# A fused attention-and-MoE kernel: the first output block of batch 0 is 8 chunks long, its weight product is made between output bursts, and no fetch slot is set

## The chip, the cores and the metric

The kernel runs on one core of one Trainium2 chip. The metric is device time in microseconds (us); runs of one kernel are summed up by their median. A span is the time from the first to the last instruction of the program in the one execution that was profiled.

## What is computed

`x` is (4, 12544, 128) in float32, `inducing` is (32, 128), `moe_w1` and `moe_w2` are (128, 1024), `moe_w_out` is (1024, 128). Cut to what matters, the reference is:

```python
def mab(q, kv):                       # per batch
    s = (q @ kv.transpose(0, 2, 1)) / sqrt(128)
    a = exp(s - s.max(-1)); a /= a.sum(-1) + 1e-9
    return a @ kv
h = mab(inducing, x)                  # (4, 32, 128): 32 queries over 12544 rows
y = mab(x, h).reshape(50176, 128)     # every row over the 32 rows of h
out = maximum(y @ w1, y @ w2) @ w_out # (50176, 128), float32
```

The kernel writes maximum(a, b) as a + relu(b - a): the part with w1 alone needs only the product w1*w_out (128x128), and the relu part needs h*(w2 - w1).

## The kernel before, in words

**Units and stages.** A batch is 98 chunks of 128 rows. Batch 0 has a stage of its own: its rows are loaded in ten units (16, 16, 16, 16, 8, 8, 8, 4, 4, 2 chunks) by DMAs that the POOL queue issues. For each unit `u_transpose` (T) makes TensorE transposes (L239) and copies them to `xT` (L244, L247), `u_scores` (S) makes exp of the scores with `inducing` (L204 to L222 for units 0 to 2, L258 and L269 for the others), and `u_accum` (A) sums the weights (L284) and the weighted rows (L293). The order of T, S and A in TensorE's queue is written out by hand for the last units. `u_h` then turns the sums into h: `sum_part` (L317), a small matmul (L324), hT4 (L334), the reciprocal rs (L343). In between stand eight transposes of w1 (L304) with their copy to `w1T` (L311). `u_hwd` makes h*(w2 - w1) in four slices of 256 columns (L441), copied out by ACT (L463) and DVE (L454) in turns.

**Blocks, bursts, finals.** Output rows are made in blocks of 16, 8, 4 or 2 chunks. `Block.stage` makes exp of the block's scores with h (L532, L542). A block is one or two parts, and a part has one to four bursts. A burst (`Part.burst`, L597) is 8 or 16 matmuls into four PSUM buffers and four relu copies (L628 on DVE, L632 on ACT). A final (`Part.final`, L659) is 16 matmuls with w_out into one PSUM buffer, with the small product `m1` opened ahead of them (L612, where a part has two column tiles) or behind them (L668), and a scaling copy on DVE into an output tile `o` (L685). Two finals fill one `o` tile (one in a block of 2 chunks); the second of them issues the tile's store to DRAM (L695), on POOL's queue for batches 0 to 2. There are four `o` tiles in turn, so the copy into a tile waits until the store from that tile four stores earlier has landed.

**The loop.** All bursts of all batches are numbered g = 0, 1, ... In step g the loop issues burst g, stages the blocks that are due, issues the oldest final that is queued, and then the jobs that are due at g. A part's finals are queued behind its last burst. Batch 0 has 49 bursts and 49 finals. From g = 7 on, final f (counted from 0) is issued in step g = f + 4.

**Which engine copies, which buffer is used.** `Model` keeps estimated times while the program is written down: it chooses the PSUM buffer that comes free first and the engine (DVE or ACT) for each relu copy. The result is a fixed order in each engine's queue.

**Jobs beside batch 0's output.** In step 9 `transpose_batch(1)` puts a one-element copy in POOL's queue (L135, waits for batch 1's last load) and seven DMA transposes of batch 1's rows in SP's queue (L129), which wait for that copy. In steps 14, 18, 22, ... `p1_scores(1, i)` (L357) reads the i-th transposed part. In step 24 `hold_loads` puts a one-element copy in POOL's queue (L143, waits for the last DMA transpose), and steps 24, 26, 28, ... put the loads of batch 2 behind it (L120), in the same queue as the stores.

**Instruction fetch.** Ahead of the fifth final, `addr_align(256, offset=174)` sets at which of 256 instruction slots TensorE's program goes on.

Of the kernel before, what the change touches and what calls it, by code (L numbers as in the profile page):

```python
# [9 lines left out]
F16 = mybir.dt.float16  # L10
# [41 lines left out]
def kernel(  # L52
# [23 lines left out]
    for i, (_, n) in enumerate(p1_blocks):  # L76
# [4 lines left out]
        else:  # L81
            units.append((i, 0, n))
    NU = len(units)
    last = NU - 4

    consts = ctx.enter_context(tc.tile_pool(name="consts", bufs=1))
# [62 lines left out]
    ones32 = consts.tile([128, 128], F32, name="ones32")  # L149
    ones16 = consts.tile([128, 1], F16, name="ones16")  # L150
    same_m = consts.tile([128, 4, M], F32, name="same_m")
    sum_scale = consts.tile([128, 2], F32, name="sum_scale")

    warm = consts.tile([128, 512], F16, name="warm")
# [11 lines left out]
    with tc.manual_schedule(engines={ET.PE, ET.DVE, ET.Activation, ET.Pool, ET.SP}):  # L166
# [28 lines left out]

        st = [dict() for _ in range(B)]

        def col_scores(b, k0, n, name):


            bi, ps = bank([128, P1B * M])
            for q in range(4):
                r = slice(32 * q, 32 * (q + 1))
                nc.tensor.matmul(  # L204
                    out=ps[r, 0 : n * 32],
                    lhsT=inducingT,
                    rhs=xT_tiles[b % 2][:, k0 : k0 + n, r],
                    start=True,
                    stop=True,
                    tile_position=(0, 32 * q),  # L210
                )
            end = model.pe(32 * n / 2400, model.bank_free[bi], "col")
            eT = eTp.tile([128, P1B * M], F16, name=f"eT_{name}", tag="eT")
            nc.scalar.activation(
                out=eT[:, 0 : n * M], in_=ps[:, 0 : n * M], func=AF.Exp, scale=scale
            )
            model.bank_free[bi] = model.ev("ACT", n * M, end)
            return eT, model.bank_free[bi]
# [11 lines left out]
        def u_transpose(i):  # L230
            t, g0, n = units[i]
            xn = xn_of(0, t)
            step = 8
            for g in range(g0, g0 + n, step):
                m = min(step, g0 + n - g)
                bi, ps = bank([128, 8, 128], F16)
                end = 0.0
                for j in range(m):
                    nc.tensor.transpose(ps[:, j, :], xn[:, g + j, :], identity16)  # L239
                    end = model.pe(0.056)  # L240
                k = p1_blocks[t][0] + g
                dst = xT_tiles[0][:, k : k + m, :]
                if i >= last - 2 or (g // step) % 2 == 0:
                    nc.vector.tensor_copy(out=dst, in_=ps[:, 0:m, :])  # L244
                    model.bank_free[bi] = model.ev("DVE", 64 * m, end)
                else:
                    nc.scalar.copy(out=dst, in_=ps[:, 0:m, :])  # L247
                    model.bank_free[bi] = model.ev("ACT", 128 * m, end)

        def u_scores(i):  # L250
            t, g, n = units[i]
            k = p1_blocks[t][0] + g
            if i < 3:
                pool0["et", i], _ = col_turn(*col_scores(0, k, n, f"0_{i}"), n, f"0_{i}")
                return
            bi, ps = bank([128, P1B * M])
            for j in range(n):
                nc.tensor.matmul(  # L258
                    out=ps[:, j * M : (j + 1) * M],
                    lhsT=xT_tiles[0][:, k + j, :],  # L260
                    rhs=inducingT,
                    start=True,
                    stop=True,
                )
                end = model.pe(0.025, model.bank_free[bi])
            et = etp.tile([128, P1B, M], F16, name=f"et_0_{i}", tag="et")
            if n % 4:
                nc.vector.memset(et[:, n : n + 4 - n % 4, :], 0.0)
            nc.scalar.activation(  # L269
                out=et[:, 0:n, :], in_=ps[:, 0 : n * M], func=AF.Exp, scale=scale  # L270
            )
            model.bank_free[bi] = model.ev("ACT", n * M, end)
            pool0["et", i] = et

        def u_accum(i):
            t, g, n = units[i]
            et = pool0.pop(("et", i))
            xn = xn_of(0, t)
            if i == 0:
                for name in ("h", "sum"):  # L280
                    pool0[name] = bank([128, 512])
                    model.bank_free[pool0[name][0]] = 1e9
            for j in range(0, n, 4):
                nc.tensor.matmul(  # L284
                    out=pool0["sum"][1][:, 0:1],
                    lhsT=et[:, j : j + 4, :],
                    rhs=ones16,
                    start=(i == 0 and j == 0),
                    stop=(i == NU - 1 and j + 4 >= n),
                )  # L290
                model.pe(0.025)
            for j in range(n):
                nc.tensor.matmul(  # L293
                    out=pool0["h"][1][:, 0:M],
                    lhsT=xn[:, g + j, :],
                    rhs=et[:, j, :],
                    start=(i == 0 and j == 0),
                    stop=(i == NU - 1 and j == n - 1),
                )
                model.pe(0.025)  # L300

        def w1T_transpose(bi, ps, jbs):
            for jb in jbs:
                nc.tensor.transpose(  # L304
                    ps[:, jb, :], w1h[:, 128 * jb : 128 * (jb + 1)], identity16
                )
                end = model.pe(0.056, model.bank_free[bi])
            return end

        def w1T_evict(bi, ps, end):  # L310
            nc.vector.tensor_copy(out=w1T, in_=ps)  # L311
            model.bank_free[bi] = model.ev("DVE", 512, end)

        def u_h():

            part = smp.tile([128, 2], F32, name="sum_part")
            nc.vector.tensor_mul(  # L317
                part, pool0["sum"][1][:, 0:1].broadcast_to((128, 2)), sum_scale
            )
            end = model.ev("DVE", 2, model.t["PE"], 0.1)  # L320
            bi, ps = pool0["sum"]
            w1T_bank = bank([128, NJB, 128], F16)
            w1T_transpose(*w1T_bank, range(NJB // 2))
            nc.tensor.matmul(  # L324
                out=ps[:, 0:2],
                lhsT=same_m.rearrange("p q m -> p (q m)"),
# [2 lines left out]
                stop=True,  # L329
            )  # L330
            end = model.pe(0.1, end)
            w1T_end = w1T_transpose(*w1T_bank, range(NJB // 2, NJB))
            hT4 = smp.tile([C, 4, M], F16, name="hT4_0", tag="hT4")
            nc.vector.tensor_scalar(  # L334
                out=hT4,
# [9 lines left out]
            hT4 = hT4.rearrange("c q m -> c (q m)")  # L345
            neg = smp.tile([C, 128], F16, name="hT4n")
            nc.scalar.mul(neg, hT4, -1.0)
            w1T_evict(*w1T_bank, w1T_end)
            st[0]["hT4"], st[0]["neg"] = hT4, neg
            st[0]["rs"], st[0]["scale"] = rs[:, 0:1], rs[:, 1:2]  # L350

# [75 lines left out]
        def u_hwd():  # L427
# [22 lines left out]
            for i, (bi, ps) in enumerate(banks):  # L450
                end = ends[i]
                sl = slice(w * i, w * (i + 1))
                if i % 2:
                    nc.vector.tensor_scalar(  # L454
                        out=hwd[:, sl],
                        in0=ps[:, 0:w],
# [242 lines left out]
        def blocks_of(b):  # L699
# [4 lines left out]
                sizes.append(s)  # L704
                rest -= s
            if b == 0:
                sizes = [2, 4, 8] + sizes[:-1]
                sizes[-1] = K - sum(sizes[:-1])
                last = sizes.pop()
                while last:  # L710
                    s = 8 if last >= 8 else 4 if last >= 4 else 2
                    sizes.append(s)
                    last -= s
# [34 lines left out]
            model.bank_free[bi] = model.ev("DVE", 128, end)  # L748


        for i in range(last - 1):
            u_transpose(i)
            if i >= 1:
                u_scores(i - 1)
            if i >= 2:
                u_accum(i - 2)
            if i < last - 2:
                keep_warm(1)
        u_transpose(last - 1)
        u_scores(last - 2)  # L760
        u_accum(last - 3)
        u_transpose(last)
        u_scores(last - 1)
        u_accum(last - 2)
        u_transpose(last + 1)
        u_scores(last)
        u_transpose(last + 2)
        u_accum(last - 1)
        u_scores(last + 1)
        u_transpose(last + 3)  # L770
        u_scores(last + 2)
        u_accum(last)
        u_scores(last + 3)
        for i in range(last + 1, NU):
            u_accum(i)
        for i in range(NP1):
# [10 lines left out]
        stages = {}  # L787
        for b in range(B):
            blks = [blk for blk in flat if blk.b == b]
            lead_in = 3 if b == 0 else 0  # L790
            for i, blk in enumerate(blks):
                j = i if i < lead_in else i - (i - lead_in) % 2
                stages.setdefault(max(-1, first[blks[j].name] - 3), []).append(blk)
        stages[-1][0].stage()
        u_hwd()
        for blk in stages[-1][1:]:
            blk.stage()
        prep_w1out()

        jobs = {}  # L800

# [31 lines left out]
            at(33 + 2 * i, sub_w, i)  # L833

        queue = []
        nfinal = 0
        for g, (p, u) in enumerate(seq):
            lead = []
            if len(queue) > 1 and queue[0][0].tn == 2 and queue[0][1] % 2 == 0:
                lead = queue[0:2]  # L840
            p.burst(u, lead)
            if g == 0:
                small_m1(0)
            for blk in stages.get(g, ()):
                blk.stage()
            if queue:
                if nfinal == 4:

                    nc.tensor.addr_align(256, offset=174, max_nops=0)
                nfinal += 1  # L850
                part, *a = queue.pop(0)
                part.final(*a)
            if u == 0 and p.t0 == 0:
# [39 lines left out]
```

## Time and profile before

| what | value |
|---|---|
| median of 7 runs | 338.3 us (337.82 to 339.77) |
| profiled execution: its time | 339.77 us |
| profiled execution: its span | 338.0 us |
| PE busy | 329.9 us, 98% of the span |
| DVE busy / ACT busy | 299.0 us / 271.8 us |
| relu copy on ACT / on DVE, 128x512 | 602 ns / 681 ns |
| scaling copy to `o`, 128x256 | 419 ns |
| DMA transposes of a batch | 21 in three batches, median 7.4 us from issue to landing |

PE is TensorE's matmul row, DVE VectorE, ACT ScalarE, POOL GpSimd and SP SyncE. In a line of the timeline the columns are the start in us from the span's start, the duration in us, the engine, the line of the kernel, the operation, what is written <- what is read, the shape and the count; in brackets stands how long the engine was idle before and what released it. A "q" behind an engine's name is its queue. In the chain of waits a line is start, duration and what the chain stood on.

### The profile page before, as it was taken

How to read it: one execution, taken by the hardware profiler on the slowest of the kernel's cores; microseconds unless marked ns; L12 is line 12 of the kernel's file. 1: busy time of each engine (PE TensorE's matmuls, PEld its weight loads, DVE VectorE, ACT ScalarE, POOL GpSimd, SP SyncE). 2: the span in 40 equal slices, each digit the busy share in tenths (PEclk: the TensorE clock that was granted, in tenths of full speed). 3: DMA queues.
4: the chain of work that ended last, by engine and by line, in shares of the span. 5: the costliest groups of instructions: out<-in, count | busy, mean ns of one | idle time of the engine just before them, and what ended most of it. 6: DMA issues, size and time to landing. Idle time of an engine off the chain costs nothing.

```text
span 338.0 us, 14462 instructions
## 1 busy us (share of the span) xinstructions
PE 329.9 (98%) x6316; PEld 262.5 (78%) x6316; DVE 299.0 (88%) x632; ACT 271.8 (80%) x523; POOL 94.5 (28%) x166
## 2 busy tenths in 40 slices
PE   8999999999999999999999999999999999999995
PEld 3776787887878878888777878888777778878875
DVE  0668999998989999999998999999998998999993
ACT  3648978777898887787899877787899989888881
POOL 6332113175741234543341232332242100000000
PEclk9999999999999999999999999999999999999999
DMA  7999799999929996994229992221221221222222
GB/s 213 208 208 214 179 200 201 203 248 222 270 104 203 212 221 145 180 252 151 81 85 172 229 248 69 97 89 70 96 96 66 106 99 68 95 95 95 96 97 109
DMA packets 54143, 51.47 MB, mean 152 GB/s; under 512 B 41536, under 2 KB 42464, under 8 KB 54080
## 3 DMA queue, kind: packets, MB, share of 16 engines
q0 software_dynamic: 11552, 32.38, 37.6%
q1 hardware_dynamic: 42528, 18.17, 26.7%
q8 instruction: 49, 0.80, 1.0%
q14 instruction: 14, 0.11, 0.1%
HBM read 28.33 MB, written 25.69 MB: 160 GB/s over the span
## 4 chain that ended last, share of the span: by engine, by line
PE 90%; DMA 3%; DVE 3%; ACT 2%; issue 1%; POOL 0%; POOLq 0%; DVEq 0%
PE ps L659 55%; PE ps L597 18%; PE ps L612 4%; DMA out_dram<-o 3%; PE ps L191 2%; PE ps L532 2%; PE ps L357 2%; PE ps L379 2%; ACT relu L632 1%; PE ps L239 1%; DVE relu L628 1%; DVE o L685 1%; ACT xT L247 1%; PE ps L553 1%; PE ps L293 1%
## 5 line engine op out<-in xcount | busy, mean ns | idle before, releaser
L632 ACT ACTIVATE relu<-ps 128x512 f16<-128x512 f32 x445 | 236.1, 602 | 42.5 <-PE ps L597 30.7
L628 DVE TENSOR_SCALAR relu<-ps 128x512 f16<-128x512 f32 x339 | 218.4, 681 | 4.3 <-PE ps L597 3.3
L659 PE MATMUL ps<-woutp,relu 128*128 128x128 f16 x3136 | 208.8, 220 | 0.1
L659 PEld LDWEIGHTS <-relu 128*128 128x128 f16 x3136 | 175.7, 98 | 31.4 <-issue 21.7
L685 DVE TENSOR_TENSOR o<-ps,rp 128x256 f32<-128x256 f32 x196 | 82.2, 419 | 17.5 <-PE ps L659 11.7
L597 PE MATMUL ps<-e,hwd 32*128 32x256 f16 (+1 forms) x1632 | 82.7, 268 | 1.0 <-DVE relu L628 0.3
L695 POOL DMA_DIRECT2D out_dram<-o x75 | 41.3, 551 | 148.2 <-DVE o L685 101.8
L597 PEld LDWEIGHTS <-hwd 32*128 32x128 f16 x1632 | 27.1, 92 | 19.6 <-issue 4.0
L612 PE MATMUL ps<-m,e 32*128 32x128 f16 x372 | 30.0, 214 | 0.8
L612 PEld LDWEIGHTS <-e 32*128 32x128 f16 x372 | 18.4, 92 | 7.1 <-issue 4.2
L399 POOL TENSOR_TENSOR eacc<-eacc,et 128x512 f32<-128x512 f32 (+1 forms) x18 | 18.5, 1029 | 0.3
L366 ACT ACTIVATE et<-ps 128x512 f16<-128x512 f32 (+1 forms) x21 | 11.5, 546 | 4.6 <-PE ps L357 4.6
L120 POOL DMA_DIRECT2D xn<-in_x_dram x21 | 11.4, 545 | 5.3 <-DMA xn<-in_x_dram 2.5
L542 ACT ACTIVATE e<-ps 128x512 f16<-128x512 f32 (+1 forms) x21 | 10.9, 579 | 0.0
L357 PE MATMUL ps<-inducingT,xT 128*128 128x32 f16 x294 | 10.6, 176 | 0.0
L379 PE MATMUL ps<-et,xn 128*128 128x32 f16 x294 | 10.6, 176 | 0.0
L357 PEld LDWEIGHTS <-xT 128*128 128x128 f16 x294 | 9.5, 96 | 0.0
L379 PEld LDWEIGHTS <-xn 128*128 128x128 f16 x294 | 9.5, 96 | 0.0
L191 PE MATMUL ps<-warm 128*128 128x512 f16 x22 | 8.3, 531 | 1.2 <-DVE warm L167 1.2
L532 PE MATMUL ps<-xT,hT 128*32 128x512 f16 (+2 forms) x120 | 8.7, 350 | 0.0
L239 PE MATMUL ps<-identity,xn 128*128 128x128 f16 x98 | 7.3, 219 | 0.7 <-issue 0.4
L244 DVE COPY xT<-ps 128x1024 f16<-128x1024 f16 (+2 forms) x10 | 5.8, 585 | 2.0 <-PE ps L239 2.0
(84 smaller groups left out, 122.1 us busy)
## 6 DMA issues: line engine op xcount, KB each, us to landing
out_dram<-o POOLq DMA_DIRECT2D x72, 256.0 KB, 4.2
xn<-in_x_dram POOLq DMA_DIRECT2D x21, 512.0 KB, 9.6
out_dram<-o SPq DMA_DIRECT2D x24, 256.0 KB, 2.0
xf<-in_x_dram SPq DMA_DIRECT2D x2, 512.0 KB, 4.1
wf<-in_moe_w_dram SPq DMA_DIRECT2D x2, 512.0 KB, 5.2
xn<-in_x_dram POOLq DMA_DIRECT2D x3, 256.0 KB, 11.0
out_dram<-o POOLq DMA_DIRECT2D x3, 128.0 KB, 5.3
xT<-xn SPq DMA_TRANSPOSE x21, 7.4
```

Source lines behind the costliest of these rows:

```text
L191: nc.tensor.matmul(out=ps, lhsT=warm[:, 0:128], rhs=warm, start=True, stop=True)
L357: nc.tensor.matmul(out=ps[:, j * M : (j + 1) * M], lhsT=xT_tiles[b % 2][:, k0 + j, :], rhs=inducingT, start=True, stop=True,)
L379: nc.tensor.matmul(out=ps[:, 0:M], lhsT=xn[:, j, :], rhs=et[:, j, :], start=(j == 0), stop=(j == n - 1),)
L399: nc.gpsimd.tensor_add(out=acc, in0=acc, in1=et[:, 0:n, :])
L532: nc.tensor.matmul(out=ps[32 * q : 32 * (q + 1), 0 : self.width], lhsT=st[self.b]["hT4"][:, 32 * q : 32 * (q + 1)], rhs=xT[:, q % self.g], ...
L597: nc.tensor.matmul(out=ps[:, jj * w : (jj + 1) * w], lhsT=st[blk.b]["hwd"][r, 128 * jb : 128 * (jb + 1)], rhs=blk.e2[r, 128 * self.t0 : 12 ...
L612: nc.tensor.matmul(out=part.fin[q][1][:, 128 * s : 128 * (s + 1)], lhsT=part.blk.e2[r, 128 * tt : 128 * (tt + 1)], rhs=st[part.blk.b]["m1" ...
L628: nc.vector.tensor_scalar(out=dst, in0=src, scalar1=0.0, scalar2=None, op0=ALU.max)
L632: nc.scalar.activation(out=dst, in_=src, func=AF.Relu)
L659: nc.tensor.matmul(out=o, lhsT=self.relu[:, jb, q, tt, :], rhs=woutp[:, jb, :], start=(start and s == 0 and jb == 0), stop=(not start and ...
L685: nc.vector.tensor_mul(self.osb[:, h : h + 2, :], ps[:, 0:256].rearrange("p (s c) -> p s c", s=2), rp.broadcast_to((128, 2, 128)),)
L695: eng.dma_start(out=outr[blk.b, :, k : k + nst, :], in_=self.osb[:, 0:nst, :])
```

## The change

Five edits are made together.

1. Batch 0 starts with a block of 8 chunks, then five of 16, then 8 and 2 (before: 2, 4, 8, five of 16, 4). One block, not three, is staged singly ahead of the others.
2. The w1 transposes with their copy (`prep_w1T`), the product w1*w_out (`prep_w1out`) and `small_m1` come behind bursts 1, 2 and 3. Before, they stood in `u_h`, behind `u_hwd` and behind burst 0.
3. The weights of units 0 to 2 are summed by ACT while it makes the exp (`accum_out`) and reduced once by DVE; twelve sum matmuls (L284) go. `sum_part` becomes one `scalar_tensor_tensor` that adds this sum.
4. The order of T, S and A: more transposes stand ahead of the sums, one warming matmul goes, and from unit 3 on all transposes are copied by DVE. In `u_hwd` DVE takes slices 0 and 2, ACT 1 and 3 (before the other way round).
5. `addr_align` goes.

```diff
-                if i >= last - 2 or (g // step) % 2 == 0:
+                if i >= NCOL or (g // step) % 2 == 0:
                     nc.vector.tensor_copy(out=dst, in_=ps[:, 0:m, :])
...
-            nc.vector.tensor_mul(
-                part, pool0["sum"][1][:, 0:1].broadcast_to((128, 2)), sum_scale
+            nc.vector.scalar_tensor_tensor(
+                out=part,
+                in0=pool0["sum"][1][:, 0:1].broadcast_to((128, 2)),
+                scalar=col_sum,
+                in1=sum_scale,
+                op0=ALU.add,
+                op1=ALU.mult,
             )
...
-            w1T_bank = bank([128, NJB, 128], F16)
-            w1T_transpose(*w1T_bank, range(NJB // 2))
...
-            w1T_end = w1T_transpose(*w1T_bank, range(NJB // 2, NJB))
...
-            w1T_evict(*w1T_bank, w1T_end)
...
-                if i % 2:
+                if i % 2 == 0:
                     nc.vector.tensor_scalar(
                         out=hwd[:, sl],
...
             if b == 0:
-                sizes = [2, 4, 8] + sizes[:-1]
-                sizes[-1] = K - sum(sizes[:-1])
-                last = sizes.pop()
+                sizes = [8] + [16] * ((K - 8) // 16)
+                last = K - sum(sizes)
...
-        for i in range(last - 1):
+        for i in range(last - 2):
...
+        steps = {"T": u_transpose, "S": u_scores, "A": u_accum}
+        for what, i in (
+            ("T", -2), ("S", -3), ("T", -1), ("A", -4), ("S", -2), ("A", -3), ("T", 0),
+            ("S", -1), ("A", -2), ("T", 1), ("T", 2), ("S", 0), ("A", -1), ("T", 3), ("S", 1),
+            ("S", 2), ("A", 0), ("S", 3),
+        ):
+            steps[what](last + i)
...
-            lead_in = 3 if b == 0 else 0
+            lead_in = 1 if b == 0 else 0
...
         u_hwd()
-        for blk in stages[-1][1:]:
-            blk.stage()
-        prep_w1out()
...
             p.burst(u, lead)
-            if g == 0:
-                small_m1(0)
+            if 1 <= g <= 3:
+                (prep_w1T, prep_w1out, lambda: small_m1(0))[g - 1]()
...
-                if nfinal == 4:
-                    nc.tensor.addr_align(256, offset=174, max_nops=0)
-                nfinal += 1
```

## The prediction

> **What bounds the kernel now.** I read the page first: busy time and the chain of waits.
>
> ```profile
> span 338.0 us, 14462 instructions
> PE 329.9 (98%) x6316; PEld 262.5 (78%) x6316; DVE 299.0 (88%) x632; ACT 271.8 (80%) x523; POOL 94.5 (28%) x166
> ...
> q8 instruction: 49, 0.80, 1.0%
> ...
> PE 90%; DMA 3%; DVE 3%; ACT 2%; issue 1%; POOL 0%; POOLq 0%; DVEq 0%
> ```
>
> The chain is not quoted whole; what matters is that TensorE sets the pace nearly everywhere, and that one piece of a DMA stands in the chain. So I looked at the chain in the opening (18 to 27 us), at the timeline where batch 1's transposes start (38 to 47 us), and at the chain and timeline around the DMA piece (69 to 84 us).
>
> The chain in the opening, after the last sums:
>
> ```profile
> 22.99 0.23 PE ps L304 x4
> 23.22 0.34 PE ps L324 x2
> 23.56 0.24 PE ps L304 x4
> 23.80 0.17 PE ps L532 x4
> 23.97 0.98 PE ps L441 x8
> 24.95 0.17 PE ps L532 x4
> 25.12 0.55 PE ps L739 x8
> 25.68 0.44 PE ps L597 x16
> ```
>
> Everything here is one queue, TensorE's: what leaves it ahead of the first burst makes the first burst earlier.
>
> The timeline around step 9:
>
> ```profile
> 38.52 0.41 DVE L685 TENSOR_TENSOR o<-ps,rp 128x256 f32<-128x256 f32 x1
> 39.23 0.54 POOL L695 DMA_DIRECT2D out_dram<-o  x1 [4.68 <-DVE o L685]
> 39.73 0.42 DVE L685 TENSOR_TENSOR o<-ps,rp 128x256 f32<-128x256 f32 x1 [0.20 <-PE ps L659]
> 39.77 0.18 POOL L135 COPY xT<-xn 1x1 f16<-1x1 f16 x1
> 39.97 25.12 SPq L129 DMA_TRANSPOSE xT<-xn  x7
> 46.42 0.56 PE L357 MATMUL ps<-inducingT,xT 128*128 128x32 f16 x16
> ```
>
> POOL's one-element copy stands behind a store, which stands behind a scaling copy on DVE. The first transpose takes 6.1 us to land (46.1); its reader L357 comes 0.3 us later. So TensorE is already nearly held by this transfer.
>
> The chain and then the timeline around the DMA piece:
>
> ```profile
> 72.63 9.71 DMA out_dram<-o
> ```
>
> ```profile
> 69.30 0.18 POOL L143 COPY xn<-xT 1x1 f16<-1x1 f16 x1 [4.35 <-PE ps L597]
> 82.47 0.42 DVE L685 TENSOR_TENSOR o<-ps,rp 128x256 f32<-128x256 f32 x1 [0.81 <-DMA out_dram<-o]
> ```
>
> A store issued at 72.63 lands 9.7 us later, because batch 2's loads stand in the same queue; DVE sits idle 0.81 us for that `o` tile. By the windows view DMA is 1.00 busy from 69 to 94 us. There the clock of progress is the queue, and its start is L143 at 69.30.
>
> **The change part by part.**
>
> *Units (edits 3, 4).* I walked the new order of the queues with the durations of the timeline: a transpose or sum issue of 8 matmuls 0.45 us, a copy to `xT` on DVE 0.65, a 128x512 exp 0.60, about 0.03 to 0.06 from an end to its reader. Twelve L284 (3 x 0.10) and a warming matmul (0.2) go, and ACT and DVE no longer meet in the copy of unit 3 (1.01 on ACT), so TensorE gets to A of unit 4 at 18.4. In the trace TensorE idles 0.42 us in the midst of unit 6's transposes, until 19.57, with "issue" as releaser and no data missing; as the rows show 49 instruction fetches of 16 KB for 12,632 matmuls and weight loads, one in about 256, I take it for a fetch. It stands at the 222nd matmul, and the 222nd matmul is now A of unit 4, so I let TensorE wait there until 19.65. From there A, T, S of units 4 to 9 take 2.7 us, ending at 22.3 instead of 22.99: **-0.7**. Without that wait it is up to 0.5 more; with it in a worse place nothing is gained: I keep 0 to -1.2. `accum_out` and the two small DVE instructions are in no row: from 0 (ACT and DVE idle there) to the nearest rows, 0.6 for a 128x512 exp and 0.17 for a small reciprocal each; I take 0, since ACT idles 1 us ahead of each exp and the fetch wait covers the rest.
>
> *From the sums to burst 0 (edits 1, 2, 4).* From the chain above L304 (0.24), the second L532 (0.17) and L739 (0.55) go: **-0.96**; the first L304 stood beside DVE's `sum_part`. The copy of w1T (0.69 on DVE) no longer stands ahead of the slices of hwd, and burst 0 of an 8-block needs slice 0 only. Burst 0 starts at 25.61 - 0.7 - 0.96 = 24.0.
>
> *Bursts 0 to 9.* The moved work does not vanish. DVE's queue from burst 0's first copy (24.4) to the scaling copy of step 9 holds 17 relu copies at 0.60 (their pitch when back to back), 6 scaling copies at 0.34, w1T 0.6, w1out 0.2, two reciprocals 0.4: 13.4 us, so 37.8 if it never waits. Following the PSUM buffers (bursts 1 to 4 each wait for a copy of the burst before or the one before that) gives about 1.3 us of idle: the copy of step 9 ends at 39.1, against 40.15 now. TensorE is then **1.0 ahead** (0.4 to 1.7).
>
> *Transposes of batch 1.* Stores now close in odd steps, since the first block holds two whole `o` tiles: L135 stands behind the store of step 9, not 8. Now: 38.94 + 0.29 + 0.54 = 39.77. Then: 39.1 + 0.83 = 40.0: **0.2 later**, though TensorE is 1.0 earlier. L357 of step 14 is reached at 45.4 and its data land at 46.3: TensorE waits 0.9, and the opening's gain is spent. The seven transposes behind it (SP's queue), wf's loads and L143 (69.5) shift by the same 0.2.
>
> *Stores and loads of batch 2.* Behind L143 the queue holds load, store, load, store as before, and is full, so landings only shift: store A at 77.9 + 0.2, store B at 82.3 + 0.2. But A now comes from steps 24, 25 and its tile is taken again in step 32 (was 33); B's in step 34 (was 35). Scaling copies now: step 32 76.64, 33 78.37, 34 79.89, 35 82.47 (81.66 without its wait). New: step 32 waits from 76.5 to 78.2; step 34, due 3.25 later at 81.45, waits to 82.47 + 0.2 = 82.7. So store B's landing, which held step 35, now holds step 34, due 79.89: 82.47 - 79.89 = 2.58; the old kernel's own loss of 0.81 goes off: 1.77; with the later L135: 1.77 + 0.2 = **+2.0**. DVE's relu copies stand behind the waiting copy, so the next burst finds no free PSUM buffer and TensorE stops too, as it did for 0.7 us now. Store C (85.6) is met at 86.0: no further wait. From batch 1 on stores close in the same steps as before.
>
> *The rest.* A stage more in batch 0 (4 matmuls, 0.24), one `dens` less, four finals with L612 in place of L668: 0 within 0.2. `addr_align`: fetches fall elsewhere. The idle rows in question are 0.42 (18.9) and 0.18 (116.2); the bounds are -0.6 (both vanish) and +1.9 (one fetch in ten, of 45, costs 0.42); I take 0, as 47 of 49 show nothing.
>
> The Trainium skill ("Runtime: NRT & Kernel Launch", Instruction fetch mechanics) says that crossing a 16 KiB block is one tail-bump, "mostly hidden". By it the 0.42 us would be no fetch, A of unit 4 would not wait, and the opening would gain some 0.5 more; by the row it would not. The sum above goes by the row.
>
> **Sum.** Span 338.0 + 2.0 = 340.0. The profiled execution took 339.77, 1.8 more than its span, so 341.8 like for like; the median shown is 1.5 below that execution, and the same difference gives 338.3 + 2.0 = **340.3**. With the opening from 0.4 to 1.7 the transposes shift from +0.8 to -0.5, and the sum runs from +1.3 to +2.6.
>
> **The rivals.**
>
> *Quicker transfers (other side).* The profiled execution is 1.5 us above the median, so its transfers may be slow ones. If transposes and loads take 12% less than in this trace (28.9 us from 39.97 to the last landing), store B lands some 3.5 us sooner, by 79, and neither kernel waits; the first transpose lands 0.7 sooner and L357 waits 0.2. Then the opening's 1.0 is kept but for that 0.2: -0.8, and -1.5 with its upper bound: 336.8 to 337.5, if the median holds no such wait either. It decides from a landing of store B before 79. For it: the gap to the median. Against: POOL's queue is busy 1.00 over 25 us, which a gap of 1.5 does not undo.
>
> *Transposes bound by the last load.* If the opening gains 2.3 and not 1.0, L135 runs right behind batch 1's last load (38.5 + 0.3), 0.96 sooner; then 1.77 - 0.96 = +0.8: 339.1. For it: no fetch wait at A of unit 4, less idle on DVE. Against: DVE's 13.4 us.
>
> *The change does not do what it says.* The units wait for fetches or loads (the last unit lands at 19.5) and copies eat the rest, so step 9 ends when it does now. Then L135 is 1.2 later: 1.77 + 1.2 = +3.0: 341.3. Against: TensorE's queue is shorter by 0.96 whatever else.
>
> **How the numbers follow.** Forecast 0.50, quicker transfers 0.20, last load 0.15, no gain 0.15. About 0.3% (1.0 us) is what a measurement of this kernel can tell from no change. Faster: three quarters of the quicker transfers, 0.15. Same: the rest of that, most of the last-load case and the edge of the forecast, 0.19. Slower: 0.66. The range, 337.3 to 341.6, leaves out about half of the quickest case and the upper third of the slowest with a late fetch or two.
>
> **What would show it.** Right: burst 0 near 24.0; L135 near 40.0; L357 of step 14 idle near 0.9; DVE idle for a landed store twice, at about 78 (1.6) and 82.7 (1.2). Wrong: L135 before 39.2, store B met without a wait, new idle "issue" rows on TensorE, or bursts 1 to 5 much slower than a copy of each engine explains.

## The result and the profile after

| | median | runs |
|---|---|---|
| changed kernel | 340.75 us (339.33 to 343.16) | 14 |
| kernel before, beside it | 338.15 us (337.64 to 339.77) | 35 |
| ratio | 1.0079, 95% interval 1.0062 to 1.0095 | |

The change costs 2.6 us. The forecast of 340.3 is close to that, but only part of its reasons held. The executions lie apart by the clock that TensorE was granted: the five with a mean clock of 1.000 took 339.33 to 339.93 us, five at 0.993 to 0.995 took 340.46 to 341.31, and five at 0.989 to 0.990 took 342.05 to 343.16. The profiled execution is one of the last five (342.36 us, clock 0.989).

The page of the changed kernel:

```profile
span 340.5 us, 14365 instructions
PE 331.0 (97%) x6267; PEld 262.7 (77%) x6267; DVE 299.0 (88%) x631; ACT 271.5 (80%) x526; POOL 94.3 (28%) x166
...
PEclk9997899999999999999999999999999999999999
...
q8 instruction: 49, 0.80, 1.0%
...
PE 87%; DMA 6%; ACT 3%; DVE 2%; POOL 1%; issue 1%; POOLq 0%
```

TensorE has 49 matmuls fewer and is busy 1.1 us longer. The row PEclk points to the reason: in two of the 40 slices (8.5 us each), from 25 to 43 us, the granted clock is below full. Before, that row was 9 throughout.

The chain in the opening of the changed kernel:

```profile
21.19 0.18 PE ps L294
21.37 0.03 issue
21.39 0.23 DVE sum_part L325
21.62 0.04 issue
21.67 0.38 PE ps L335 x2
22.05 0.22 PE ps L541 x4
22.28 0.56 PE ps L450 x4
```

The L304, the second L532 and the L739 of the old chain are gone, and burst 0 starts at 23.19. The timeline of the same kernel a little later shows the slow clock at work:

```profile
29.62 0.40 PE L621 MATMUL ps<-m,e 32*128 32x128 f16 x4 [0.77 <-ACT m L508]
29.95 1.89 PE L668 MATMUL ps<-woutp,relu 128*128 128x128 f16 x16
...
32.40 1.89 PE L668 MATMUL ps<-woutp,relu 128*128 128x128 f16 x16
```

A final's 16 matmuls took 1.07 us in the kernel before; here they take 1.89. The timeline where batch 1's transposes start and are read:

```profile
40.69 0.42 DVE L694 TENSOR_TENSOR o<-ps,rp 128x256 f32<-128x256 f32 x1
...
41.41 0.54 POOL L704 DMA_DIRECT2D out_dram<-o  x1 [1.99 <-DVE o L694]
41.95 0.18 POOL L136 COPY xT<-xn 1x1 f16<-1x1 f16 x1
...
48.57 0.55 PE L366 MATMUL ps<-inducingT,xT 128*128 128x32 f16 x16 [0.79 <-DMA xT<-xn]
```

L136 (L135 before) is at 41.95, not 39.77, and the first reader of a transpose waits 0.79 us for it. The timeline around the output tiles that the forecast expected to be late:

```profile
67.46 0.18 POOL L144 COPY xn<-xT 1x1 f16<-1x1 f16 x1 [1.89 <-PE ps L668]
...
78.96 0.42 DVE L694 TENSOR_TENSOR o<-ps,rp 128x256 f32<-128x256 f32 x1
...
82.51 0.42 DVE L694 TENSOR_TENSOR o<-ps,rp 128x256 f32<-128x256 f32 x1
```

These are the scaling copies of steps 32 and 34. No bracket stands behind them: neither waits for a store. In the trace the seven transposes take 25.2 us from the first issue to the last landing (28.9 in the profile before), and store B, issued at 71.51, lands at 79.53 and not at 82.5.

### The profile page after: what moved, and what is told of

The parts are those of the page before. It is cut to its first block, busy times and chain, and to the rows that moved or that the text cites. A ratio compares the mean times of both kernels' runs of the same rounds, so it can differ in the third digit from the quotient of the medians.

```text
span 340.5 us, 14365 instructions
## 1 busy us (share of the span) xinstructions
PE 331.0 (97%) x6267; PEld 262.7 (77%) x6267; DVE 299.0 (88%) x631; ACT 271.5 (80%) x526; POOL 94.3 (28%) x166
## 4 chain that ended last, share of the span: by engine, by line
PE 87%; DMA 6%; ACT 3%; DVE 2%; POOL 1%; issue 1%; POOLq 0%
PE ps L668 55%; PE ps L606 18%; PE ps L621 5%; DMA xn<-in_x_dram 4%; ACT relu L641 2%; PE ps L366 2%; PE ps L388 2%; PE ps L541 2%; DMA xT<-xn 2%; DVE relu L637 1%; DVE o L694 1%; POOL xn L126 1%; PE ps L562 1%; PE ps L482 0%; PE ps L246 0%
## 5 line engine op out<-in xcount | busy, mean ns | idle before, releaser
L668 PEld LDWEIGHTS <-relu 128*128 128x128 f16 x3136 | 177.6, 98 | 32.0 <-issue 22.5
L606 PEld LDWEIGHTS <-hwd 32*128 32x128 f16 x1600 | 26.3, 92 | 19.2 <-issue 3.5
L621 PE MATMUL ps<-m,e 32*128 32x128 f16 x380 | 31.3, 216 | 1.5 <-ACT m L508 0.8
L366 PE MATMUL ps<-inducingT,xT 128*128 128x32 f16 x294 | 10.6, 176 | 0.8 <-DMA xT<-xn 0.8
L366 PEld LDWEIGHTS <-xT 128*128 128x128 f16 x294 | 9.5, 96 | 0.9 <-issue 0.9
L541 PE MATMUL ps<-xT,hT 128*32 128x512 f16 (+2 forms) x116 | 8.5, 356 | 0.0
L194 PE MATMUL ps<-warm 128*128 128x512 f16 x21 | 7.3, 497 | 1.2 <-DVE warm L170 1.2
```

Of the source, the lines that this page charges most:

```text
L366: nc.tensor.matmul(out=ps[:, j * M : (j + 1) * M], lhsT=xT_tiles[b % 2][:, k0 + j, :], rhs=inducingT, start=True, stop=True,)
L541: nc.tensor.matmul(out=ps[32 * q : 32 * (q + 1), 0 : self.width], lhsT=st[self.b]["hT4"][:, 32 * q : 32 * (q + 1)], rhs=xT[:, q % self.g], ...
L606: nc.tensor.matmul(out=ps[:, jj * w : (jj + 1) * w], lhsT=st[blk.b]["hwd"][r, 128 * jb : 128 * (jb + 1)], rhs=blk.e2[r, 128 * self.t0 : 12 ...
L621: nc.tensor.matmul(out=part.fin[q][1][:, 128 * s : 128 * (s + 1)], lhsT=part.blk.e2[r, 128 * tt : 128 * (tt + 1)], rhs=st[part.blk.b]["m1" ...
L668: nc.tensor.matmul(out=o, lhsT=self.relu[:, jb, q, tt, :], rhs=woutp[:, jb, :], start=(start and s == 0 and jb == 0), stop=(not start and ...
```

## The experiments

Two theories were set against each other. **Clock**: the new bursts 1 to 4 leave TensorE too thin, its clock is halved, and that is the loss. **Late transfers**: what is lost is decided by batch 1's transposes and their reader. For run 1 both forecast the same time, so there the clock tells them apart, not the time. A third question was the fetch slot. The kernel before was run beside each of the three sets; its median there was 337.90, 338.02 and 337.97 us.

**1. Fill the thin bursts.** In the changed kernel, two matmuls on the warming tile are put ahead of each of bursts 1 to 4, into the PSUM buffer that the burst then overwrites.

```diff
-            def burst(self, u, lead=()):
+            def burst(self, u, lead=(), fill=0):
...
+                for _ in range(fill):
+                    nc.tensor.matmul(
+                        out=banks[0][1], lhsT=warm[:, 0:128], rhs=warm, start=True, stop=True
+                    )
...
-            p.burst(u, lead)
+            p.burst(u, lead, 2 if 1 <= g <= 4 else 0)
```

> The changed kernel, with two more matmuls of the warming tile ahead of each of bursts 1 to 4, into the burst's own first PSUM buffer, which the burst then overwrites; everything else stands in the same order. Clock theory (TensorE has so little to do in bursts 1 to 4 that its clock is granted at 0.5 for up to 6.8 us from 29 us on): clock 1.000 in nearly every run, median near 339.7 us (the changed kernel's runs at clock 1.000 took 339.3 to 339.9), runs within 1 us of each other. Late-transfer theory (stores close one step later, so batch 1's transposes and batch 2's loads hold TensorE): the 1.6 us above the kernel before stay, so 339.7 too, and L366 of step 14 still waits some 0.9 us; it gives no reason why the clock should change. Fetch-slot theory: 340.75 us, nothing moves.

Measured: 339.25 us (338.77 to 339.80), ratio 1.0040 (1.0026 to 1.0054); the clock is 1.000 in all six runs. Eight matmuls more make the kernel 1.5 us quicker. The windows view shows how the changed kernel got to its slow clock. It is cut into stretches of 3.413 us, half the time for which the clock was at half. They are counted from the place where the warming matmuls at the kernel's start begin to follow one another every 0.22 us instead of every 0.43 us: 5.39 us into the span in the changed kernel, 6.14 us with the fill. Seven stretches from 5.39 us end at 29.28 us, where the clock falls, and nine end at 36.11 us, where it is back (columns: window, its length, busy time of PE, PEld, DVE, ACT and POOL with counts, granted clock, DMA share, GB/s):

```profile
22.44:25.85 3.41, 3.19 (x48) 1.72 (x47) 3.12 (x7) 3.38 (x8) 0.53 (x1) 1.00 1.07 212
25.85:29.26 3.41, 2.43 (x33) 1.15 (x31) 3.30 (x7) 3.41 (x8) 0.00 (x0) 1.00 1.06 214
29.26:32.67 3.41, 3.05 (x35) 2.43 (x35) 1.69 (x5) 1.46 (x5) 1.19 (x2) 0.50 1.05 211
32.67:36.08 3.41, 3.41 (x39) 2.90 (x37) 2.27 (x4) 2.14 (x5) 0.60 (x1) 0.50 1.06 214
```

And the same view with the fill:

```profile
26.60:30.01 3.41, 2.73 (x39) 1.40 (x37) 3.41 (x7) 3.41 (x8) 0.68 (x2) 1.00 1.06 214
30.01:33.42 3.41, 3.41 (x71) 2.84 (x72) 2.87 (x7) 2.37 (x6) 0.95 (x2) 1.00 1.07 215
```

A stretch with TensorE busy for 2.43 us is followed by half the clock; one with 2.73 us is not. Busy time alone does not decide it, though. In run 9 below, a stretch on the same kind of grid (counted from 5.19 us) has less, and the clock stays:

```profile
35.91:39.32 3.41, 2.23 (x38) 1.62 (x35) 2.41 (x5) 2.26 (x5) 0.98 (x3) 1.00 0.80 227
39.32:42.73 3.41, 2.94 (x59) 2.39 (x61) 2.51 (x5) 2.16 (x4) 0.28 (x1) 1.00 0.84 195
```

What the hardware counts as busy is therefore open; that the fill keeps the clock is shown. In the thin stretch of the changed kernel ACT is busy 3.41 of 3.41 us and DVE 3.30. TensorE waits there for the relu copies of the first bursts, for the staging, and for the copies of w1T and m1 that edit 2 put between the bursts.

But 1.35 us of loss stay, and the fill's timeline shows the other theory at work:

```profile
39.02 0.18 POOL L136 COPY xT<-xn 1x1 f16<-1x1 f16 x1 [0.17 <-DMA xn<-in_x_dram]
...
45.54 0.55 PE L366 MATMUL ps<-inducingT,xT 128*128 128x32 f16 x16 [0.87 <-DMA xT<-xn]
```

The copy no longer waits for a store but for batch 1's last load, and L366 waits 0.87 us.

**2. Half the fill, with the transposes' job in step 8**, `2 if 1 <= g <= 4` becoming `1 if ...`.

> The run with the copies and transposes behind step 8 and the extra matmuls, but one a burst instead of two. Clock theory with the bounds that the runs give (of a stretch of 3.41 us, TensorE was busy 2.18, 2.38 and 2.43 us in three runs whose next stretch was halved, and 2.73 us with two matmuls a burst, whose next stretch was not): one matmul of 0.21 us for each of the two or three bursts in that stretch makes about 2.45 to 2.6, so the point lies here: if the clock stays at 1.000 the time is 339.0 us, if not the runs lie apart, those below a clock of 0.996 at 340.3 us or more. Rival (the extra matmuls help in another way than by the clock): halfway between, clock 1.000 and 339.5 to 340.0 us.

Measured: 339.31 us (338.98 to 340.29), clock 0.998 to 1.000. TensorE was busy 2.81 us in the stretch in question and the clock stayed: clock theory, but 0.3 us above its time and with more busy time in that stretch than the expectation worked out.

**3. The same fill, late**: `2 if 5 <= g <= 8`, in the changed kernel.

> The changed kernel with the two extra matmuls ahead of bursts 5 to 8 instead of 1 to 4: the same extra work, later. Clock theory (what halves the clock is the thin work before 29.3 us): the clock falls to 0.5 from about 29.3 us as in the changed kernel; the halved stretch may end one step sooner (3.4 us instead of 6.8), so 340.0 to 341.5 us with clocks of 0.989 to 0.995. Rival (any extra matmuls in the first steps do it, or it is the order of PSUM buffers they change): 339.25 us at a clock of 1.000, as with bursts 1 to 4.

Measured: 341.72 us (340.73 to 343.35), ratio 1.0116 (1.0092 to 1.0139). The rival (any extra matmuls help) falls: nothing is gained. Three runs at 0.994 to 0.995 took 342.27 to 343.35, three at 0.999 to 1.000 took 340.73 to 341.17; the upper ones are above what was expected, probably because late matmuls stand on a full TensorE and cost their own time (not measured by itself). The profiled run is one of the latter three:

```profile
25.27:28.68 3.41, 2.84 (x43) 1.34 (x42) 3.30 (x7) 3.41 (x8) 0.00 (x0) 1.00 1.07 215
28.68:32.09 3.41, 2.65 (x44) 1.64 (x43) 2.39 (x6) 2.16 (x6) 1.18 (x2) 1.00 1.07 214
```

Here the stretches fall elsewhere against the same bursts: the thin part is shared out on two of them, 2.84 and 2.65 us, and the clock stays. A stretch cut at 26.40 us in this same trace would hold only 2.14 us, less than the 2.43 that were followed by half the clock; so it counts where the fixed stretches begin. That the changed kernel's own runs differ for this reason is argued from this view, not shown run by run.

**4. The new blocks alone** (edit 1 in the kernel before), **and 5. the new blocks with the fill.**

```diff
-                sizes = [2, 4, 8] + sizes[:-1]
-                sizes[-1] = K - sum(sizes[:-1])
-                last = sizes.pop()
+                sizes = [8] + [16] * ((K - 8) // 16)
+                last = K - sum(sizes)
...
-            lead_in = 3 if b == 0 else 0
+            lead_in = 1 if b == 0 else 0
```

> The kernel before with the new blocks of batch 0 alone (8, five of 16, 8, 2; one staged singly), edit 1 alone: units, w1 transposes, w1*w_out, m1 and addr_align as before. Late-transfer theory: stores close in odd steps, the copy that releases batch 1's transposes stands behind the store of step 9, and no gain of the units pays for it: L357 of step 14 waits near 0.9 us and a scaling copy near 75 to 85 us waits for a landed store or the loads bound it; 339.7 to 341.2 us. Clock theory: four bursts without a final between them leave TensorE idle as in the changed kernel, so part of the runs show a clock below 1.000 and 340 us or more; with the clock at 1.000 it would be 338.2. Fetch-slot theory: 338.2 us.

> The kernel before with the new blocks alone (341.6 us, clock 0.990, halved for 6.8 us from 30.9) and the two extra matmuls ahead of bursts 1 to 4. Clock theory: the halved stretch goes; runs of the changed kernel at a clock of 1.000 were about 2.9 us quicker than those at 0.990, so 338.7 us at a clock of 1.000. Rival (what the new blocks cost is their later copies and transposes, L135 at 43.68 instead of 39.77, and the clock is an aside): the clock is 1.000 and the time still 340.5 us or more.

Measured: 341.60 us (340.52 to 342.57) alone, clock 0.990 to 0.994, halved for 6.8 us from 30.9; 339.50 us (339.26 to 339.66) with the fill, clock 0.999 to 1.000. So edit 1 by itself brings the halved clock and more than the whole loss, and 2.1 us of it are the clock. The signs that the late-transfer theory named for run 4 are not in its profile: the reader L357 and the scaling copies of steps 30 to 37 have no wait for a transfer. The fill did not bring run 5 down to 338.7: neither theory's number was met, and 1.5 us above the kernel before stay without a slow clock.

**6. The transposes' job a step earlier**, with the fill of 1: `t0, l0 = (9, 24)` becomes `(8, 24)`.

> The changed kernel with the two extra matmuls ahead of bursts 1 to 4 (which kept the clock at 1.000 and gave 339.25 us) and with the copies and transposes of batch 1 put behind the store of step 8 instead of step 9. Theory (a late transfer is what is left of the loss): the 0.87 us for which the scores of step 14 waited for their transpose (landed 45.41) go, since the first transpose lands about one step (1.3 us) earlier; time 338.4 us, span about 336.2. Rival (the transposes are held by something else, the loads or the previous stores): they land where they did, the wait stays at 0.6 to 0.9 and the time at 339.2 us.

Measured: 339.22 us (338.29 to 340.22): the rival. L366 waits only 0.21 us, but its data land at 45.63 (45.41 without the edit); TensorE merely came 0.9 us later in this execution, because the opening was slower (a wait of 0.80 us at the sums, at 18.6, though the exp named in the row had ended at 19.00 and the wait at 19.38). L136 moved from 39.02 to 38.70 only: batch 1's last load lands at 38.65.

Two numbers from each trace put all these kernels side by side: the start of burst 15, which stands right behind the first reader of a transpose, and the time from there to the end.

| kernel (profiled execution) | burst 0 | first transpose lands | its reader waits | burst 15 | from there to the end |
|---|---|---|---|---|---|
| before (shown first) | 25.61 | 46.03 | 0 | 46.90 | 291.07 |
| before, profiled again (12) | 24.55 | 45.63 | 0.31 | 46.25 | 290.13 |
| before, six output tiles (11) | 24.72 | 44.25 | 0 | 45.95 | 290.16 |
| before, no slot (8) | 24.71 | 45.58 | 0 | 46.20 | 290.71 |
| changed, old blocks (10) | 24.94 | 45.43 | 0 | 46.17 | 290.42 |
| changed with fill (1) | 22.86 | 45.41 | 0.87 | 46.03 | 290.98 |
| half the fill, step 8 (2) | 23.11 | 45.52 | 0.74 | 46.14 | 290.98 |
| fill, step 8 (6) | 23.75 | 45.63 | 0.21 | 46.25 | 291.11 |
| fill, step 8, slot (9) | 23.20 | 45.70 | 0 | 47.31 | 291.04 |
| fill late (3) | 23.36 | 47.56 | 0.81 | 48.18 | 291.22 |
| blocks alone (4) | 25.48 | 49.16 | 0 | 49.84 | 290.96 |
| blocks with fill (5) | 24.66 | 45.43 | 0 | 46.73 | 291.02 |
| changed with slot (7) | 23.18 | 46.60 | 0 | 47.49 | 290.97 |
| changed | 23.19 | 48.44 | 0.79 | 49.05 | 291.40 |

Wherever the reader waits, burst 15 starts 0.6 us after the transpose lands. In runs 1, 2 and 6 that is at 46.03 to 46.25, whether burst 0 starts at 22.86 or at 23.75: batch 1's last load (38.4 to 39.0) and the first transpose behind it (6.2 to 6.9 us from issue) hold it there. The old order gets there at 45.95 to 46.25 from a burst 0 at 24.55 to 24.94, mostly without a wait. So the earlier opening bought nothing; that an earlier transfer would let it through was not run. And every kernel with the new blocks needs 0.8 to 1.1 us more from burst 15 on than the 290.13 of run 12 (1.27 in the changed one, which has a wait of 0.30 for "issue" at 147.6 as well). TensorE has no idle time of note in it: steps 24 to 34 take 16.82 us (16.25 before), and eight staging matmuls (L541) stand in them where the old order has none; steps 34 to 60 take 0.3 more. Up to step 24 the new order has made 16 staging matmuls of batch 0 and the old one 20. So staging moved behind the place where TensorE has to wait, into steps where it is full; that accounts for the 0.57 us of steps 24 to 34. The 0.3 us are not traced to a cause: from burst 15 to the end run 1 has 5589 matmuls and run 12 has 5597.

**7 to 9. The fetch slot**: set again in the changed kernel (7), taken out of the kernel before (8), and set again with the fill and step 8 (9).

```diff
+                if nfinal == 4:
+                    nc.tensor.addr_align(256, offset=174, max_nops=0)
+                nfinal += 1
```

> The changed kernel with addr_align(256, offset=174) ahead of the fifth final again, that is with edit 5 undone alone. Fetch-slot theory: most of the 2.6 us goes, 338.5 to 339.5 us. Clock theory and late-transfer theory: 340.75 us within 0.7, and clocks between 0.989 and 1.000 as now, since the opening is the same.

> The kernel before without addr_align, edit 5 alone. Fetch-slot theory: 339.2 us or more. Clock theory and late-transfer theory: 338.15 us within 0.4, clock 1.000.

> The same kernel with the fetch slot of the kernel before set again ahead of its fifth final. If the lost slot costs in the changed kernel what its removal alone cost in the kernel before (about 1.2 us in the median), the time is 337.2 us where the kernel without the slot is at 338.4. Rival: in the changed order the fetches fall elsewhere, and none of TensorE's waits over 0.25 us was one for nothing the profile shows in the run with the extra matmuls; then the slot gives nothing, or loses up to 0.45 us to a wait of the kind seen at 39.97 us in the changed kernel with the slot: 338.4 to 338.9 us.

Measured: 340.29 us (339.84 to 340.97) for 7, where the clock and late-transfer theories put it; 339.14 (337.82 to 340.77), ratio 1.0035 (1.0015 to 1.0056), for 8, near the fetch-slot theory; 339.84 (339.76 to 340.12) for 9, above both of its forecasts. Without the slot the kernel before loses some 1.2 us in the median and scatters over 3 us; its profile has one "issue" wait, 0.33 us at 71.55, and its worst runs are unexplained. In the new order the old slot is no cure: with the fill it is 0.6 us slower than none (9 against 6), without the fill 0.5 us quicker, among runs that the clock sets apart (7 against the changed kernel). The profile of 9 has this:

```profile
39.80 0.40 PE L610 MATMUL ps<-e,hwd 32*128 32x256 f16 x7 [1.66 <-issue]
```

TensorE stands still for 1.66 us, waiting for nothing that the profile shows; that this is an instruction fetch is argued, not shown. Burst 15 starts at 47.31 there, and nothing follows to take the 1.06 us back. In 7 the clock was below 0.996 in four of six runs and TensorE was late anyway (burst 15 at 47.49).

**10. The other edits with the old blocks**: the changed kernel with edits 1 and 2 undone, `prep_w1T` right behind `u_hwd`.

```diff
-                sizes = [8] + [16] * ((K - 8) // 16)
-                last = K - sum(sizes)
+                sizes = [2, 4, 8] + sizes[:-1]
+                sizes[-1] = K - sum(sizes[:-1])
+                last = sizes.pop()
...
         u_hwd()
+        prep_w1T()
+        for blk in stages[-1][1:]:
+            blk.stage()
+        prep_w1out()
...
-            if 1 <= g <= 3:
-                (prep_w1T, prep_w1out, lambda: small_m1(0))[g - 1]()
+            if g == 0:
+                small_m1(0)
```

> The changed kernel with the old blocks 2, 4, 8 and with w1 times w_out made ahead of the bursts as before: what is left of the change is the order of the units, the sums made by ScalarE, the swapped scalings and the missing fetch slot. Theory (the front is a real gain, the blocks are the loss): burst 0 starts near 23.2 us instead of 25.6, the clock stays 1.000, and two thirds or more of the 2.4 us reach the end: 337.9 - 1.6 + 1.2 for the missing slot = 337.5 us or less. Rival (an earlier start is taken back in the first steps, since ScalarE and VectorE set their pace): 338.5 to 339.2 us, as the kernel before without its slot (339.14).

Measured: 339.53 us (338.39 to 342.02), ratio 1.0054 (1.0031 to 1.0077), above both forecasts. It does not settle what it was meant to: burst 0 starts at 24.94, because TensorE now waits 0.62 us for the copy of w1T ahead of it, so the early opening is not in this kernel. Its profiled execution has burst 15 at 46.17 and 290.42 from there. Why its runs scatter over 3.6 us stays open; four of the twelve have a clock of 0.995 (339.43 to 342.02), so a clock below full can come with the old blocks too, but runs at 1.000 lie as far apart.

**11. Six output tiles** in the kernel before (`bufs=4` becomes `bufs=6` in the pool `outp`), **and 12. the kernel before profiled again.**

> The kernel before with six output tiles instead of four, so that no scaling copy of steps 30 to 48 can wait for a store. If the waits for stores that its profile showed (VectorE 0.81 us at 82.47, the step after it 0.69 us longer) are part of its usual time, the time falls by 0.7 us or more to 337.2 us or less. Rival (they belonged to the one profiled execution; no other run's profile had one at that step): 337.9 us, as the kernel before.

> The kernel before, profiled again: whether the profile that the forecast was worked out from (time 339.77 us, against a median of 338.3) is a usual execution. If the wait for a landed store at 82.47 is usual, VectorE waits 0.4 us or more near that step again and step 34 to step 49 takes 25.0 us; if not, these steps take 24.3 us and the span is near 336.1 us.

Measured: 337.94 us (337.67 to 338.90), ratio 0.9996 (0.9985 to 1.0007), for 11; 338.26 (337.69 to 340.59) for 12, whose profile has a span of 336.4. The timeline of 12 at the place of the 0.81 us wait (step 35):

```profile
79.22 0.41 DVE L685 TENSOR_TENSOR o<-ps,rp 128x256 f32<-128x256 f32 x1
...
80.89 0.41 DVE L685 TENSOR_TENSOR o<-ps,rp 128x256 f32<-128x256 f32 x1
```

No wait; the store in question landed at 76.47, 4.4 us before its tile was taken again, and steps 34 to 49 took 24.26 us (25.01 in the profile shown first). The wait belonged to one execution, whose transposes took 28.9 us and not the 23.8 to 26.6 of all other profiles.

None of these kernels beats the kernel before.

## Why the forecast was right, and where it was not

- **The opening (burst 0 at 24.0).** 23.19, and 22.86 to 23.75 with the fill. Against the usual execution of the kernel before (24.55) that is 1.4 us earlier, near the 1.7 of the sum; of the 2.4 against the profile shown first, 1.1 belongs to that execution, its wait of 0.42 until 19.57 among it, which is not there in run 12 (run 4 has 0.39 at the same place). The fetch wait put at A of unit 4 is not in the changed kernel's profile (it waited 0.56 us for a load, until 18.12); a wait at that place, 0.80 us, is in run 6. So it comes and goes.
- **Bursts 0 to 9 (TensorE 1.0 ahead, 1.3 us of idle).** This step failed. The idle between bursts was sized nearly right (1.56 us, burst 0 to burst 9), and where the fill keeps the clock TensorE is 0.9 ahead at burst 9 (36.15, against 37.06 in run 12). But the sum has no term for what the idle sets off: half the clock for 6.83 us. Burst 9 of the changed kernel starts at 39.26, and L136 is at 41.95. This is the largest single piece of the 2.6 us: 1.5 us by run 1, 2.1 by runs 4 and 5.
- **L135 near 40.0, L357 waiting 0.9, the gain spent.** The core of it held. In runs 1, 2 and 6, at full clock, L136 is at 38.4 to 39.0, behind the last load and not behind the store, but the reader waits 0.74 and 0.87 us in runs 1 and 2 (0.21 in run 6, whose opening was late) and the opening is lost there. The case "transposes bound by the last load" had the right releaser.
- **Store B, +2.0.** This step failed, and it carried the number. It was read from an execution with slow transfers. The rival "quicker transfers" named this: 12% less time for the transposes (25.4 instead of 28.9 us) and neither kernel waits. That is what the runs show: they took 23.8 to 26.6 us, store B landed at 77.1 to 80.2 in the kernels with the new blocks, and step 34 never waited for it. Only the rival's time (336.8 to 337.5) was wrong, since it kept the opening's gain and knew of no slow clock.
- **The rest, 0 within 0.2.** Mis-sized: +0.85 us from burst 15 on in run 1, of which 0.57 us stand where staging moved into a full TensorE. "A stage more" was a misreading as well: batch 0 now has eight blocks and not nine, and the trace 116 staging matmuls (L541) and not 120 (L532).
- **`addr_align`, 0 within -0.6 and +1.9.** Taking it out of the kernel before costs some 1.2 us; putting it back in the new order gains 0.5 us or loses 0.6. It can't be added to the other terms.

So the +2.0 was luck: the wait for stores that carried it is in no profile with the new blocks, and "store B met without a wait", one of the forecast's own signs of being wrong, came true. In its place stand other things: with the opening's gain spent, 0.9 from burst 15 on, and roughly 1 to 3 us for the clock, nothing in the runs whose clock stayed. Some 0.5 us between the fill's median and its profiled execution is not accounted for; the missing slot, which run 8 prices at 1.2 us in the old order, may have a part in it, though run 9 did not win it back.

## What to carry to other kernels

Before an opening is made earlier, look for the first transfer that a later step reads: if TensorE will wait there anyway, work ahead of it is free and work moved behind it is not. When matmuls are spread thin, look at the granted clock stretch by stretch, not only at the sum of the gaps. And profile the kernel before twice: a wait in one execution may not be in the next, and here the larger part of the forecast stood on one.

## What the runs showed of the hardware

- TensorE's clock was halved after a stretch of 3.41 us in which it was busy 2.18 (run 7), 2.38 (run 4) or 2.43 us (changed kernel), and not after 2.65, 2.73, 2.81 or 2.84 in the same part of runs 3, 1 and 2. Elsewhere less did not halve it: 2.23 us in run 9 (35.91 to 39.32) and 2.54 us in run 1 (43.69 to 47.10). So these runs give no limit for the busy time.
- In every profile with a halved clock the fall comes a whole number of 3.413 us stretches after the clock's first rise: seven in the changed kernel (5.39 and 29.28), in run 7 (5.64 and 29.53) and in run 4 (7.04 and 30.94). It stayed at half for one or two such stretches (3.4 us in run 7, 6.8 in the changed kernel and run 4). The longest single gap in or beside the changed kernel's thin stretch was the 0.77 us that ended at 29.62; in it were others of 0.2 and 0.3 us.
- The Trainium skill ("TensorE: Matmul & The Clock Gate", What's actually happening) states a free-running activity window of 3413 ns, and that the point of change depends on where in it the work falls; the lengths here agree (3.41 and 6.83 us at half, 23.89 us from the first rise to the fall), and the runs of one kernel with and without a halved clock fit it. The same page (HAM oscillation) gives the rule of no gap over about 3.4 us. These runs differ from that rule: gaps of 0.2 to 0.8 us were enough. Its section on psum-queue depth-cycling, which speaks of frequent short idles between groups of matmuls, fits better.
- With a fetch slot set, TensorE stood still once for 1.66 us, for nothing that the profile shows (run 9); the single waits of this kind in the other profiles are at most 0.42 us.
- `accum_out` adds an instruction of its own on ACT, ACTIVATION_READ_ACCUMULATOR, 0.20 us, three of them here.
